# Attention and two MoE layers on one core: first tiles in pieces, squares summed two tiles wide, products planned one matmul at a time

## The chip, the core and the metric

The kernel runs on one core of one Trainium2 chip. The core's engines are TensorE (PE; its weight loads are listed apart as PEld), VectorE (DVE), ScalarE (ACT), GpSimd (POOL, hardly used here) and SyncE (SP, which issues transfers). The metric is the time of one launch on the device in microseconds. Of the kernel before there are three runs: 1128.27 us in the median, 1125.93 to 1128.51.

## What is computed

`q`, `k` and `v` are 6016 x 256 in f32. The attention is over the channels, so its score matrix is only 256 x 256, and its output is the input of two dense layers:

```python
qn = q / (np.linalg.norm(q, axis=1, keepdims=True) + 1e-06)   # norm of each channel, over all tokens
kn = k / (np.linalg.norm(k, axis=1, keepdims=True) + 1e-06)
s = kn.transpose(0, 2, 1) @ qn / tau
a = softmax(s)
x = v @ a                                                     # 6016 x 256
rms = np.sqrt(np.mean(x * x, axis=-1, keepdims=True) + 1e-06)
xn = x / rms * rms_g
g, val = xn @ w_gate, xn @ w_val                              # 1536 wide
y = (silu(g) * val) @ w_out                                   # first MoE
h = y @ w_in                                                  # 2048 wide
out = (h - np.tanh(h)) @ w_out2                               # second MoE
```

## The kernel before

**Attention.** The 6016 tokens are 47 tiles of 128 rows. `attention()` groups them in 12 chunks: the first four tiles in pieces of 1, 1 and 2 tiles (FIRST_PIECES), ten whole chunks of four tiles, and three last tiles as 2 and 1. A tile of q or k is 128 x 256 f32, so a piece of two is 128x512 and a whole chunk 128x1024 in the rows. SP's queue issues all loads of q and those of k but the three pieces of k's first chunk, which go through ScalarE's queue. For each tile and each half m of the channels, `score()` adds one f32 matmul k-tile x q-tile to S[m] in PSUM: 94 matmuls. An f32 matmul leaves two records in the trace, a matmul of the layers below one. Before the first S, TensorE multiplies WARM = 11 dummies of ones into `nrm`. In the last four chunks (BEHIND) all S[0] come first and S[1] last.

**Sums of squares.** The norms need the sum of q^2 and of k^2 over all tokens. ScalarE squares each piece (`sq`); the first chunk goes right into `acc`, [128, 2, 4, 256], four tiles wide for q and for k. VectorE adds every later square to it, 1024 columns in one instruction. Towards the end (FOLDED = 2) it folds `acc` from four tiles to one, and folds the last squares before it adds them. TensorE then multiplies `acc` by ones into `nrm` (two matmuls for q, s = 0, two for k, s = 1). VectorE makes 1/norm of it (n_, y_, t_, r_, 128x8 each), TensorE spreads it (`rq_ps`), and the softmax gives `a`, from which x = v @ a follows.

**Layers.** A layer's hidden columns come in units (6 of the gate and 6 of the value for each of five pairs of token blocks in the first MoE, p = 1 to 5, 30 of each; 48 in the second). `unit()` forms a product of 2 x 2 blocks with seven products, in the PSUM banks X, T, Y and Z: X gets A11*B11, T gets S1*T1, ScalarE copies X to Y and T to m5, Y gets S2*T2, VectorE adds Z = Y + m5, X gets A12*B21, Y gets S3*T3, Z gets S4*B22 and Y gets A22*T4. In the rows a trailing g, v or h names the gate, value or second layer: Yv<-T2h,sh is the first matmul that adds S2*T2 to Y of a value unit, on top of the copy Yv<-Xv. Each product is made of f32 parts, high and low (wh, wl, xh, xl): three matmuls wh*xh, wl*xh, wh*xl of up to 512 columns, in `prod()`. The outputs `acc<-uc` collect the second half of each layer; they fill the time between.

**The order.** A planner in Python (`Graph`) decides it when the kernel is built. Each `g.op` is an instruction with a cost, its operands and, for TensorE, a key; `run()` goes through time with LATENCY between engines, takes on TensorE the ready instruction with the least key, and on the others the one that has to be done first by the round before (`late`); `schedule()` keeps the best of ROUNDS = 6. A `prod` is one instruction of the plan: its three matmuls stand together and it is ready when all four parts are. Each engine then runs its list in order, waiting on semaphores. The field `slack` adds to a transfer's planned end only.

Of the kernel before, what the change touches and what calls it, by code (L numbers as in the profile page):

```python
# [16 lines left out]
P = 128  # L17
# [96 lines left out]
class Graph:  # L114
# [38 lines left out]
    def run(self):  # L153
# [12 lines left out]

        def now_known(o):
            heappush(known[o.eng], (o.ready, o.idx))
            if o.eng != "SP":
                for s, data in o.succs:  # L170
                    if s.left == 1 and s.eng != o.eng and s.eng in PATIENT:
                        soon[s.eng].append((o.ready + o.cost + self.gap(o, s, data), s.idx))
# [113 lines left out]
ROUNDS = 6  # L286
FIRST_PIECES, LAST_PIECES = [1, 1, 2], [2, 1]
FOLDED, BEHIND = 2, 4
WARM = 11
LAG0, LAG1, LAG2 = 4100.0, 9500.0, 4800.0  # L290
# [4 lines left out]
def attn_moe_kernel(  # L295
# [129 lines left out]
    def prod(out, w, x, n, start, key=None):  # L425

        (wh, wl), (xh, xl) = w, x

        def emit():
            o = ap(out)  # L430
            for i, (a, b) in enumerate(((wh, xh), (wl, xh), (wh, xl))):
                nc.tensor.matmul(  # L432
                    o, ap(a), ap(b), start=start and i == 0, stop=i == 2, skip_group_check=True)

        return g.op("PE", 3 * (n / 2.4 + 13.7), emit, [wh, wl, xh, xl], [out], key=key)

    def matmul(out, a, b, n, start, stop, full=True, key=None, **kw):
        return g.op(
            "PE", n * (4 if full else 1) / 2.4 + (5 if full else 13.7),
            lambda: nc.tensor.matmul(ap(out), ap(a), ap(b), start=start, stop=stop, **kw),  # L440
            [a, b], [out], key=key)

    def rsqrt(m, y, t, cols):
# [231 lines left out]
    def attention():  # L675
        CH = 4
        chunks, t = [], 0
        for pieces in [FIRST_PIECES] + [[CH]] * ((NT - CH - sum(LAST_PIECES)) // CH) + [LAST_PIECES]:
            chunks.append((t, [(sum(pieces[:x]), n) for x, n in enumerate(pieces)]))
            t += sum(pieces)  # L680
# [6 lines left out]
        kr = k.rearrange("(p n) c -> p n c", p=P)  # L687
        acc = new(head, "acc", "acc", [P, 2, CH, C])
        S = [bank(ACC[0][m], f"S{m}") for m in range(KC)]
# [3 lines left out]
        def load(i):  # L693
# [3 lines left out]
            for j, n in pieces:  # L697
                for s, src in enumerate((qr, kr)):
                    r, size = raw[i][s], n * C * P * 4
                    from_ = src[:, t0 + j:t0 + j + n, :]  # L700
                    to = r.view(lambda t, j=j, n=n: t[:, j:j + n, :], j)
                    if s and i == 0:
                        g.op("SP", 0, lambda to=to, a=from_: nc.scalar.dma_start(
                            out=to.ap, in_=a), (), [to], size=size)
                    else:
                        last_score[:] = [dma(to, from_, size, (), [to])]
# [18 lines left out]
        for i, (t0, pieces) in enumerate(chunks):  # L725
            load(i)
            sqs = [None] * 2
            if i:
                for s in range(2):
                    pool, tag = ((head, "sq"), (act, "wraw"), (act, "vl"))[(2 * i + s) % 3]  # L730
                    sqs[s] = new(pool, tag, f"sq{i}_{s}", [P, CH, C])
            for j, n in pieces:
                for s in range(2):
                    src = raw[i][s].view(lambda t, j=j, n=n: t[:, j:j + n], j)
                    if i == 0:
                        activation(sums(s, lambda t, s=s, j=j, n=n: t[:, s, j:j + n]), src,
                                   AF.Square, n * C)
                        continue

                    def sq(x, n):  # L740
                        return sqs[s].view(lambda t, j=j: t[:, j + x:j + x + n], j)

                    activation(sq(0, n), src, AF.Square, n * C)
                    if i < NCH - FOLDED:
                        a = sums(s, lambda t, s=s: t[:, s])
                        add(a, a, sq(0, n), n * C)
                        continue
                    for h in (2, 1):
                        if n >= 2 * h:
                            add(sq(0, h), sq(0, h), sq(h, h), h * C)  # L750
                    a = sums(s, lambda t, s=s: t[:, s, 0])
                    add(a, a, sq(0, 1), C)
            if i == NCH - FOLDED - 1:
                for s in range(2):
                    for h in (2, 1):
                        add(sums(s, lambda t, s=s, h=h: t[:, s, :h]),
                            sums(s, lambda t, s=s, h=h: t[:, s, :h]),
                            sums(s, lambda t, s=s, h=h: t[:, s, h:2 * h]), h * C)
            if i < NCH - BEHIND:
# [16 lines left out]
        for s in range(2):  # L776
            for m in range(KC):
                c0 = 2 * (KC * s + m)
                matmul(nrm[:, c0:c0 + 2],
                       sums(s, lambda t, s=s, m=m: t[:, s, 0, m * P:(m + 1) * P]),  # L780
                       ones[:, :2], 2 * 24, True, True, key=0.0)
        n_, y_, t_, r_ = (new(head, x, f"{x}_", [P, NN]) for x in "nytr")
# [10 lines left out]
        for m in range(KC):  # L793
            matmul(rq_ps[:, m * P:(m + 1) * P],
                   r_.view(lambda t, m=m: t[:, 2 * m:2 * m + 1].to_broadcast([P, P])), ident, P,
                   True, True, key=0.0)
        rq = rr("rq")
# [576 lines left out]
```

## Time and profile before

| | us |
|---|---|
| median of 3 runs | 1128.27 |
| lowest, highest | 1125.93, 1128.51 |
| the profiled execution | 1126.14 |
| its span in the trace | 1124.3 |
| TensorE busy | 1118.2 |
| VectorE busy | 815.1 |
| ScalarE busy | 695.2 |

The span is shorter than the execution by 1.84 us. A matmul's record goes on while the next has begun: at 512 columns a record is 0.39 us long, and the next starts about 0.23 us after it. The distance from start to start tells more than the busy time.

### The profile page before, as it was taken

To read this page: it belongs to the slowest core of one execution; us is meant where nothing else is said; L and a number is where in the kernel's file an instruction comes from. 1 tells how busy PE (TensorE), PEld (TensorE's weight loads), DVE (VectorE), ACT (ScalarE), POOL (GpSimd) and SP (SyncE) were. 2 spreads that over 40 slices of the span, in tenths; PEclk is the share of its full clock that TensorE was granted. 3 is DMA by queue.
4 is the path that set the end of the run, shared out by engine and by line. 5 is a ranking of instruction groups with operands and counts; after the bars stand their busy time and mean duration, and the time that the engine had idled before them with its cause. 6 is when DMAs were issued, how large, how long until landed. Compare 5 with 4: busy or idle time off the path is not lost.

```text
span 1124.3 us, 14173 instructions
## 1 busy us (share of the span) xinstructions
PE 1118.2 (99%) x4986; PEld 926.7 (82%) x4986; DVE 815.1 (72%) x1360; ACT 695.2 (62%) x1203; POOL 0.7 (0%) x6
## 2 busy tenths in 40 slices
PE   9999999999999999999999999999999999999998
PEld 8778888878888888888788899888888888888887
DVE  5889866786779578547865877867767768667664
ACT  6675556566656655555655766756656656656654
POOL 0000000000000000000000000000000000000000
PEclk9999999999999999999999999999999999999999
DMA  9765112224332320100221300101100101100101
GB/s 352 288 205 170 57 64 64 67 66 128 116 88 73 113 85 19 56 16 19 72 67 45 92 36 12 59 1 29 47 1 29 48 1 29 38 1 1 38 1 38
DMA packets 41771, 76.74 MB, mean 68 GB/s; under 512 B 6874, under 2 KB 12250, under 8 KB 41700
## 3 DMA queue, kind: packets, MB, share of 16 engines
q1 hardware_dynamic: 41268, 75.31, 20.3%
q8 instruction: 39, 0.64, 0.2%
q10 hardware_dynamic: 432, 0.52, 0.1%
q14 instruction: 32, 0.26, 0.1%
HBM read 54.02 MB, written 21.80 MB: 67 GB/s over the span
## 4 chain that ended last, share of the span: by engine, by line
PE 96%; DMA 3%; DVE 1%; ACT 0%; issue 0%; SPq 0%; ACTq 0%
PE acc L432 40%; PE Yh L432 9%; PE Yv L432 6%; PE Xh L432 6%; PE Yg L432 6%; PE Xg L432 4%; PE Xv L432 4%; PE Zh L432 3%; PE Th L432 3%; PE g L432 3%; PE v L432 3%; DMA q<-q_in 2%; PE x L432 2%; PE Tv L432 2%; PE Tg L432 2%; PE Zv L432 2%
## 5 line engine op out<-in xcount | busy, mean ns | idle before, releaser
L413 DVE TENSOR_TENSOR ulc<-wc,uc 128x512 fp32r<-128x512 f32 (+1 forms) x192 | 130.2, 679 | 89.2 <-ACT uc L394 87.1
L394 ACT ACTIVATE uc<-wc 128x512 fp32r<-128x512 f32 (+1 forms) x192 | 119.6, 624 | 102.0 <-PE acc L432 86.6
L394 ACT ACTIVATE uc<-tc 128x512 fp32r<-128x512 f32 x120 | 73.8, 630 | 99.8 <-DVE tc L409 95.3
L413 DVE TENSOR_TENSOR ulc<-tc,uc 128x512 fp32r<-128x512 f32 x120 | 79.9, 684 | 3.5 <-ACT uc L394 2.6
L409 DVE TENSOR_TENSOR Zv<-Yv,m5v 128x512 f32<-128x512 f32 x30 | 20.9, 696 | 49.3 <-PE Yv L432 49.3
L409 DVE TENSOR_TENSOR wc<-Xh,wc 128x512 f32<-128x512 f32 (+1 forms) x48 | 32.5, 677 | 19.7 <-ACT wc L394 19.4
L394 ACT ACTIVATE wc<-Xh 128x512 f32<-128x512 f32 (+1 forms) x48 | 28.2, 587 | 28.8 <-PE Xh L432 28.6
L440 PE MATMUL S<-q,k 128*128 128x256 f32 x188 | 42.4, 384 | 0.4 <-DMA k<-k_in 0.4
L409 DVE TENSOR_TENSOR Zh<-Yh,m5h 128x512 f32<-128x512 f32 (+1 forms) x48 | 32.9, 686 | 10.8 <-ACT m5h L394 10.4
L440 PEld LDWEIGHTS S<-q,k 128*128 128x128 f32 x188 | 35.8, 193 | 5.8 <-issue 0.8
L409 DVE TENSOR_TENSOR wc<-Yh,wc 128x512 f32<-128x512 f32 (+1 forms) x48 | 32.5, 678 | 9.6 <-ACT wc L394 9.6
L394 ACT ACTIVATE wc<-Yh 128x512 f32<-128x512 f32 (+1 forms) x48 | 28.1, 586 | 14.2 <-PE Yh L432 13.5
L394 ACT ACTIVATE tc<-Xg 128x512 f32<-128x512 f32 x30 | 17.9, 597 | 29.7 <-PE Xg L432 29.7
L394 ACT ACTIVATE m5h<-Th 128x512 f32<-128x512 f32 (+1 forms) x48 | 28.2, 588 | 12.0 <-PE Th L432 12.0
L394 ACT ACTIVATE Yh<-Xh 128x512 f32<-128x512 f32 (+1 forms) x48 | 27.6, 575 | 11.6 <-PE Xh L432 9.7
L394 ACT ACTIVATE r<-acc 128x512 f32<-128x512 f32 (+2 forms) x48 | 27.5, 591 | 9.4 <-PE acc L432 9.0
L409 DVE TENSOR_TENSOR s<-Yh,m5h 128x512 f32<-128x512 f32 (+1 forms) x48 | 32.5, 676 | 0.1
L409 DVE TENSOR_TENSOR acc<-acc,sq 128x1024 f32<-128x1024 f32 (+1 forms) x24 | 24.4, 1023 | 11.1 <-ACT sq L394 10.1
L409 DVE TENSOR_TENSOR wc<-s,wc 128x512 f32<-128x512 f32 (+1 forms) x48 | 32.3, 673 | 0.2
L409 DVE TENSOR_TENSOR wc<-Zh,wc 128x512 f32<-128x512 f32 (+1 forms) x48 | 32.2, 671 | 0.0
L409 DVE TENSOR_TENSOR tc<-Yg,m5g 128x512 f32<-128x512 f32 x30 | 20.6, 687 | 15.9 <-PE Yg L432 15.7
L394 ACT ACTIVATE tc<-Zg 128x512 f32<-128x512 f32 x30 | 17.9, 596 | 23.0 <-PE Zg L432 18.9
(923 smaller groups left out, 3495.1 us busy)
## 6 DMA issues: line engine op xcount, KB each, us to landing
vraw<-vT_in SPq DMA_DIRECT2D x11, 512.0 KB, 5.1
y<-r SPq DMA_DIRECT2D x22, 256.0 KB, 2.0
q<-q_in SPq DMA_DIRECT2D x10, 512.0 KB, 8.7
k<-k_in SPq DMA_DIRECT2D x10, 512.0 KB, 9.4
y<-y SPq DMA_DIRECT2D x20, 256.0 KB, 2.6
outT<-r SPq DMA_DIRECT2D x20, 256.0 KB, 2.0
raw<-w_in_in SPq DMA_DIRECT2D x8, 512.0 KB, 4.4
raw<-w_out_in SPq DMA_DIRECT2D x8, 512.0 KB
```

The costliest lines, as they stand in the source:

```text
L394: nc.scalar.activation(out=ap(out), in_=ap(in_), func=func, **{x: ap(a) for x, a in kw.items()})
L409: return dve(lambda: f(out=ap(out), in0=ap(a), in1=ap(b)), n, 2, [a, b], [out])
L413: lambda: nc.vector.tensor_sub(out=ap(out), in0=ap(in_), in1=f32(ap(hi))), n, 2,
L432: nc.tensor.matmul(o, ap(a), ap(b), start=start and i == 0, stop=i == 2, skip_group_check=True)
L440: lambda: nc.tensor.matmul(ap(out), ap(a), ap(b), start=start, stop=stop, **kw),
```

## The change

`FIRST_PIECES` is a list of three chunks: 1, 1, 2; then 2, 2; then 2, 2. k's piece of two tiles in the first chunk goes to SP's queue. `WARM` is 6. `acc` is two tiles wide; only the first two tiles are squared into it, all others are added two tiles at a time, and no square or sum is folded on VectorE. The `nrm` matmuls are four for q and four for k, in pairs that add the two tiles of `acc`. The first `nrm` matmul of each and the first of `rq_ps` carry a slack of 700, by which the planner takes them for ready later. `prod()` makes three instructions of the plan in place of one, each with only its own two operands.

```diff
@@ now_known
+            if o.eng != "SP":
+                o.ready += o.slack
@@
-FIRST_PIECES, LAST_PIECES = [1, 1, 2], [2, 1]
-FOLDED, BEHIND = 2, 4
-WARM = 11
+FIRST_PIECES, LAST_PIECES = [[1, 1, 2], [2, 2], [2, 2]], [2, 1]
+BEHIND = 4
+WARM = 6
+MARGIN = 700.0
@@ prod
-        def emit():
-            o = ap(out)
-            for i, (a, b) in enumerate(((wh, xh), (wl, xh), (wh, xl))):
-                nc.tensor.matmul(
-                    o, ap(a), ap(b), start=start and i == 0, stop=i == 2, skip_group_check=True)
-        return g.op("PE", 3 * (n / 2.4 + 13.7), emit, [wh, wl, xh, xl], [out], key=key)
+        for i, (a, b) in enumerate(((wh, xh), (wl, xh), (wh, xl))):
+            g.op("PE", n / 2.4 + 13.7, lambda i=i, a=a, b=b: nc.tensor.matmul(
+                ap(out), ap(a), ap(b), start=start and i == 0, stop=i == 2,
+                skip_group_check=True), [a, b], [out], key=key)
@@ matmul
+        o.slack = slack
+        return o
@@ attention
-        acc = new(head, "acc", "acc", [P, 2, CH, C])
+        acc = new(head, "acc", "acc", [P, 2, 2, C])
-                    if s and i == 0:
+                    if s and i == 0 and j < 2:
                         g.op("SP", 0, lambda to=to, a=from_: nc.scalar.dma_start(
@@
+                    def part(x, n):
+                        return sums(s, lambda t, s=s: t[:, s, x:x + n])
@@
                     activation(sq(0, n), src, AF.Square, n * C)
-                    if i < NCH - FOLDED:
-                        a = sums(s, lambda t, s=s: t[:, s])
-                        add(a, a, sq(0, n), n * C)
-                        continue
-                    for h in (2, 1):
-                        if n >= 2 * h:
-                            add(sq(0, h), sq(0, h), sq(h, h), h * C)
-                    a = sums(s, lambda t, s=s: t[:, s, 0])
-                    add(a, a, sq(0, 1), C)
+                    for x in range(0, n, 2):
+                        w = min(2, n - x)
+                        add(part(0, w), part(0, w), sq(x, w), w * C)
@@ nrm
-                matmul(nrm[:, c0:c0 + 2],
-                       sums(s, lambda t, s=s, m=m: t[:, s, 0, m * P:(m + 1) * P]),
-                       ones[:, :2], 2 * 24, True, True, key=0.0)
+                for x in range(2):
+                    matmul(nrm[:, c0:c0 + 2],
+                           sums(s, lambda t, s=s, m=m, x=x: t[:, s, x, m * P:(m + 1) * P]),
+                           ones[:, :2], 2 * 24, x == 0, x == 1, key=0.0,
+                           slack=0 if m or x else MARGIN)
```

TensorE around the norms, as it stands before (S_178 and S_185 are the two halves of S, the tiles named 253 to 292 belong to the last chunks):

```order
L440 MATMUL S_178<-q_253,k_257 128x256 x4
L440 MATMUL S_178<-q_274,k_277 128x256 x2
L440 MATMUL nrm<-ones,acc 128x2 x2
L440 MATMUL S_178<-q_274,k_277 128x256
L440 MATMUL nrm<-ones,acc 128x2 x2
L440 MATMUL S_178<-q_274,k_277 128x256
L440 MATMUL S_178<-q_292,k_296 128x256 x3
L440 MATMUL S_185<-q_233,k_238 128x256 x4
L440 MATMUL S_185<-q_253,k_257 128x256 x4
L440 MATMUL S_185<-q_274,k_277 128x256
L440 MATMUL rq_ps<-ident,r__428 128x128 x2
L440 MATMUL S_185<-q_274,k_277 128x256 x3
```

The same place after (the halves are S_161 and S_168, the last chunks 263 to 307):

```order
L439 MATMUL S_161<-q_263,k_269 128x256 x4
L439 MATMUL S_161<-q_286,k_290 128x256
L439 MATMUL nrm<-ones,acc 128x2 x4
L439 MATMUL S_161<-q_286,k_290 128x256 x2
L439 MATMUL nrm<-ones,acc 128x2 x4
L439 MATMUL S_161<-q_286,k_290 128x256
L439 MATMUL S_161<-q_307,k_313 128x256 x3
L439 MATMUL S_168<-q_243,k_246 128x256 x4
L439 MATMUL S_168<-q_263,k_269 128x256 x2
L439 MATMUL rq_ps<-ident,r__438 128x128 x2
L439 MATMUL S_168<-q_263,k_269 128x256 x2
L439 MATMUL S_168<-q_286,k_290 128x256 x4
```

q's sums stand one S matmul earlier and are four matmuls instead of two; two S matmuls instead of one stand between q's and k's; the spread `rq_ps` has ten S matmuls between it and k's sums instead of thirteen.

VectorE in the chain from the norms to their reciprocal, before (gv0y and w10y are weights of the layers being prepared, 1024 wide):

```order
L461 SCALAR_TENSOR_TENSOR t__399<-y__394,n__392 128x8
L464 TENSOR_TENSOR t__399<-t__399,y__394 128x8
L526 TENSOR_SCALAR gv0y<-gv0y 128x1024
L465 SCALAR_TENSOR_TENSOR y__394<-t__399,y__394 128x8
L531 SCALAR_TENSOR_TENSOR gv0y<-gv0raw,gv0y 128x1024
L786 TENSOR_TENSOR y__394<-y__394,n__392 128x8
L536 SCALAR_TENSOR_TENSOR gv0y<-gv0raw,gv0y 128x1024
L787 TENSOR_SCALAR y__394<-y__394 128x8
L788 TENSOR_SCALAR y__394<-y__394,tau_t 128x4
L790 RECIPROCAL r__428<-y__394 128x8
```

And after:

```order
L462 SCALAR_TENSOR_TENSOR t__418<-y__415,n__413 128x8
L465 TENSOR_TENSOR t__418<-t__418,y__415 128x8
L466 SCALAR_TENSOR_TENSOR y__415<-t__418,y__415 128x8
L781 TENSOR_TENSOR y__415<-y__415,n__413 128x8
L782 TENSOR_SCALAR y__415<-y__415 128x8
L783 TENSOR_SCALAR y__415<-y__415,tau_t 128x4
L527 TENSOR_SCALAR gv0y<-gv0y 128x1024
L785 RECIPROCAL r__438<-y__415 128x8
L532 SCALAR_TENSOR_TENSOR gv0y<-gv0raw,gv0y 128x1024
L537 SCALAR_TENSOR_TENSOR gv0y<-gv0raw,gv0y 128x1024
```

The three wide instructions on gv0y stood between the short ones; two of them now stand behind the reciprocal, and the first just ahead of it.

TensorE in a unit of the second MoE (X is A11\*B11, T is S1\*T1, Y gets S2\*T2 on the copy of X), before:

```order
L432 MATMUL Xh_7976<-B11l,l20h 128x512
L432 MATMUL acc_7399<-uc_7891,l26h 128x512
L432 MATMUL acc_7399<-uc_7891,l26l 128x512
L432 MATMUL acc_7399<-ulc_7898,l26h 128x512
L432 MATMUL acc_7405<-uc_7891,l26h 128x512
L432 MATMUL acc_7405<-uc_7891,l26l 128x512
L432 MATMUL acc_7405<-ulc_7898,l26h 128x512
L432 MATMUL Th_7998<-T1h,l2s_5104 128x512 x2
L432 MATMUL Th_7998<-T1l,l2s_5104 128x512
L432 MATMUL Yh_7987<-T2h,l2s_5104 128x512 x2
L432 MATMUL Yh_7987<-T2l,l2s_5104 128x512
```

And in a unit after:

```order
L432 MATMUL Xh_8443<-B11l,l25h 128x512
L432 MATMUL Th_8460<-T1h,l2s_5786 128x512 x2
L432 MATMUL Th_8460<-T1l,l2s_5786 128x512
L432 MATMUL acc_8128<-uc_8406,l24h 128x512
L432 MATMUL Yh_8464<-T2h,l2s_5786 128x512 x2
L432 MATMUL Yh_8464<-T2l,l2s_5786 128x512
L432 MATMUL Xh_8443<-B21h,l25h 128x512
L432 MATMUL Xh_8443<-B21h,l25l 128x512
L432 MATMUL Xh_8443<-B21l,l25h 128x512
L432 MATMUL acc_8128<-uc_8406,l24l 128x512
L432 MATMUL acc_8128<-ulc_8415,l24h 128x512
L432 MATMUL Yh_8464<-T3h,l25h 128x512
```

Between the last matmul of X with B11 and the first of Y with T2 there were six outputs and three of T; in this unit of after there are three of T and one output, and five matmuls between Y's last with T2 and its first with T3.

## Rows read from the trace of the kernel before

**Rows 1.** The page: busy time of engines, chain that ended last.
```profile
PE 1118.2 (99%) x4986; PEld 926.7 (82%) x4986; DVE 815.1 (72%) x1360; ACT 695.2 (62%) x1203; POOL 0.7 (0%) x6
...
PE 96%; DMA 3%; DVE 1%; ACT 0%; issue 0%; SPq 0%; ACTq 0%
```

**Rows 2.** By stage: window, length, busy, granted clock, DMA share, GB/s.
```profile
0.00:5.94 5.94, 4.86 (x22) 4.86 (x23) 0.54 (x3) 2.63 (x5) 0.70 (x6) 1.00 0.60 188
...
10.72:39.07 28.35, 28.35 (x131) 24.98 (x132) 26.32 (x29) 21.85 (x23) 0.00 (x0) 1.00 1.03 400
...
155.50:633.90 478.40, 478.33 (x2082) 387.90 (x2081) 338.72 (x596) 288.78 (x511) 0.00 (x0) 1.00 0.23 70
```

**Rows 3.** Waits of TensorE and its weight load: total, times, longest, us.
```profile
PE nrm L440 <- DVE ones L483: 1.1, 1, 1.1
PE nrm L440 <- DVE acc L409: 0.9, 1, 0.9
PE S L440 <- DMA k<-k_in: 0.4, 1, 0.4
...
PEld Yv L432 <- ACT Yv L394: 7.1, 17, 0.5
...
PEld Yg L432 <- ACT Yg L394: 1.2, 5, 0.3
...
PEld Yh L432 <- DVE Zh L409: 0.9, 4, 0.3
```

**Rows 4.** TensorE's timeline of the head: start, duration, idle before.
```profile
1.08 5.07 PE L440 MATMUL nrm<-ones 128*128 128x128 f32 x22 [1.08 <-DVE ones L483]
5.94 4.34 PE L440 MATMUL S<-q,k 128*128 128x256 f32 x16
10.72 28.73 PE L440 MATMUL S<-q,k 128*128 128x256 f32 x132 [0.44 <-DMA k<-k_in]
40.31 0.61 PE L440 MATMUL nrm<-ones,acc 128*128 128x2 f32 x4 [0.86 <-DVE acc L409]
40.78 0.68 PE L440 MATMUL S<-q,k 128*128 128x256 f32 x2
```

**Rows 5.** ScalarE's timeline of the squares, first and last.
```profile
4.38 0.40 ACT L394 ACTIVATE acc<-k 128x256 f32<-128x256 f32 x1
7.96 0.63 ACT L394 ACTIVATE acc<-q 128x512 f32<-128x512 f32 x1 [3.18 <-DMA q<-q_in]
8.50 0.61 ACT L394 ACTIVATE acc<-k 128x512 f32<-128x512 f32 x1
...
35.78 1.14 ACT L394 ACTIVATE sq<-q 128x512 f32<-128x512 f32 x2
```

**Rows 6.** VectorE's timeline of the fold.
```profile
33.27 0.69 DVE L409 TENSOR_TENSOR acc<-acc 128x512 f32<-128x512 f32 x1
...
39.84 1.28 DVE L409 TENSOR_TENSOR acc<-acc,sq 128x256 f32<-128x256 f32 x3
```

**Rows 7.** One of 17 stalls: ScalarE, weight load and TensorE, 241 to 244.
```profile
242.12 0.58 ACT L394 ACTIVATE Yv<-Xv 128x512 f32<-128x512 f32 x1
...
242.75 0.19 PEld L432 LDWEIGHTS Yv<-T2h,sh 128*128 128x128 f32 x1 [0.41 <-ACT Yv L394]
...
242.75 0.50 PE L432 MATMUL Yv<-T2h,sh 128*128 128x512 f32 x1
```

**Rows 8.** A unit of the second MoE, 767 to 772.
```profile
767.26 0.39 PE L432 MATMUL Xh<-B11l,l26h 128*128 128x512 f32 x1
...
767.68 0.58 ACT L394 ACTIVATE Yh<-Xh 128x512 f32<-128x512 f32 x1 [0.27 <-PE Xh L432]
...
769.98 0.39 PE L432 MATMUL Yh<-T2l,l2s 128*128 128x512 f32 x1
...
770.48 0.70 DVE L409 TENSOR_TENSOR Zh<-Yh,m5h 128x512 f32<-128x512 f32 x1 [0.30 <-ACT m5h L394]
...
771.57 0.39 PE L432 MATMUL Yh<-T3h,l26h 128*128 128x512 f32 x1
```

More of the change, by code (lines that the diff above doesn't have):

```diff
@@ L427, in prod, with matmul @@
         (wh, wl), (xh, xl) = w, x
-        def emit():
-            o = ap(out)
-            for i, (a, b) in enumerate(((wh, xh), (wl, xh), (wh, xl))):
-                nc.tensor.matmul(
-                    o, ap(a), ap(b), start=start and i == 0, stop=i == 2, skip_group_check=True)
-        return g.op("PE", 3 * (n / 2.4 + 13.7), emit, [wh, wl, xh, xl], [out], key=key)
-    def matmul(out, a, b, n, start, stop, full=True, key=None, **kw):
-        return g.op(
+        for i, (a, b) in enumerate(((wh, xh), (wl, xh), (wh, xl))):
+            g.op("PE", n / 2.4 + 13.7, lambda i=i, a=a, b=b: nc.tensor.matmul(
+                ap(out), ap(a), ap(b), start=start and i == 0, stop=i == 2,
+                skip_group_check=True), [a, b], [out], key=key)
+    def matmul(out, a, b, n, start, stop, full=True, key=None, slack=0, **kw):
+        o = g.op(
             "PE", n * (4 if full else 1) / 2.4 + (5 if full else 13.7),
@@ L677, in attention @@
         chunks, t = [], 0
-        for pieces in [FIRST_PIECES] + [[CH]] * ((NT - CH - sum(LAST_PIECES)) // CH) + [LAST_PIECES]:
+        whole = (NT - len(FIRST_PIECES) * CH - sum(LAST_PIECES)) // CH
+        for pieces in FIRST_PIECES + [[CH]] * whole + [LAST_PIECES]:
             chunks.append((t, [(sum(pieces[:x]), n) for x, n in enumerate(pieces)]))
@@ L727, in attention @@
             sqs = [None] * 2
[L728 to L731, printed above, removed]
+            for s in range(2):
+                pool, tag = ((head, "sq"), (act, "wraw"), (act, "vl"))[(2 * i + s) % 3]
+                sqs[s] = new(pool, tag, f"sq{i}_{s}", [P, CH, C])
             for j, n in pieces:
@@ L734, in attention @@
                     src = raw[i][s].view(lambda t, j=j, n=n: t[:, j:j + n], j)
-                    if i == 0:
-                        activation(sums(s, lambda t, s=s, j=j, n=n: t[:, s, j:j + n]), src,
-                                   AF.Square, n * C)
+                    def part(x, n):
+                        return sums(s, lambda t, s=s: t[:, s, x:x + n])
+                    if i == 0 and j < 2:
+                        assert n == 1
+                        activation(part(j, 1), src, AF.Square, C)
                         continue
                     def sq(x, n):
-                        return sqs[s].view(lambda t, j=j: t[:, j + x:j + x + n], j)
+                        return sqs[s].view(lambda t, x=j + x: t[:, x:x + n], j)
                     activation(sq(0, n), src, AF.Square, n * C)
-                    if i < NCH - FOLDED:
-                        a = sums(s, lambda t, s=s: t[:, s])
-                        add(a, a, sq(0, n), n * C)
-                        continue
-                    for h in (2, 1):
-                        if n >= 2 * h:
-                            add(sq(0, h), sq(0, h), sq(h, h), h * C)
-                    a = sums(s, lambda t, s=s: t[:, s, 0])
-                    add(a, a, sq(0, 1), C)
[L753 to L758, printed above, removed]
+                    for x in range(0, n, 2):
+                        w = min(2, n - x)
+                        add(part(0, w), part(0, w), sq(x, w), w * C)
             if i < NCH - BEHIND:
@@ L795, in attention @@
                    r_.view(lambda t, m=m: t[:, 2 * m:2 * m + 1].to_broadcast([P, P])), ident, P,
-                   True, True, key=0.0)
+                   True, True, key=0.0, slack=0 if m else MARGIN)
         rq = rr("rq")
```

## The prediction, made before the changed kernel had run

> **What bounds the kernel now.** I read the page first. TensorE is busy 99% of the span and holds 96% of the chain that ended last; VectorE and ScalarE are at 72% and 62% [rows 1]. So only two things can move the end: the number and length of TensorE's own records, and the few places where it stands. The second view is the one by stage [rows 2]: in the first MoE (155.5 to 633.9 us) TensorE is busy 478.33 of 478.40 us, so busy time cannot show what is lost there, since a matmul whose weights come late counts as busy. A longer record shows it. That is why I read the waits third, of TensorE and of its weight load apart [rows 3]: TensorE has three waits in all, 1.1 us for the first constant, 0.9 for the sum of squares, 0.4 for k; the weight load waits 7.1 us for ScalarE's copy of Yv, 17 times, and some 2 us in two other short ones. Fourth come the timelines of the head [rows 4 to 6]: dummies from 1.08, S from 5.94, `nrm` at 40.31. All sums are made against the profiled execution, 1126.14 us (span 1124.3, 1.84 around it); the median of the runs is 1128.27, and a difference found here is put on 1128.27.
>
> **Fewer dummies, pieces.** First the clock. 22 dummy records of 128 columns take 5.94 - 1.08 = 4.86 us, 0.221 each; an f32 record of S has 256 columns and takes 28.73/132 = 0.218 [rows 4]. So the dummies run at the lower level, 1.2 GHz, and S later at 2.4, though the column of the granted clock says 1.00 for both stretches [rows 2]. A record of S at the low level is taken as twice 0.218, 0.43. With 12 dummy records S can start at 1.08 + 12 x 0.221 = 3.73; its operands are there by then or just behind (ScalarE squares k1, the last of the first two tiles, at 4.38 with three squares queued ahead of it [rows 5]). Tiles 0 and 1 are 8 records: 3.4 us, done at 7.2. Then S needs q2 and k2. They were squared at 7.96, after 3.18 us of waiting for the DMA, and at 8.50 [rows 5]. The same bytes are ahead of them after, so I take k2 at 8.3, and TensorE stands about 1.1 us there. In before it stood again for the first whole chunk's k, till 10.72 [rows 4]; that chunk now comes in halves, the first needing half the bytes, so I expect S to run on from 8.3. 138 S records stand between this and `nrm`: 8.3 + 138 x 0.218 = 38.4, against 10.72 + 28.73 = 39.45 in before. That is 1.1 us earlier, of which 0.43 is one S matmul that now stands behind `nrm`.
>
> **The sums of squares.** In before TensorE then waited 0.86 us for `acc` and started `nrm` at 40.31 [rows 4], since VectorE was folding: its last three short adds alone run from 39.84 to 41.12 [rows 6]. After, a whole square needs two 512-wide adds of at most 0.69 [rows 6], 1.38 together with their start-up, and arrives every 512 KB / 400 GB/s = 1.31 us [rows 2]; VectorE is about level with it, without folds. The last q squares end at 35.78 + 1.14 = 36.9 [rows 5]; behind them I count one add of k's chunk (0.69) and q's own last one (0.43, a third of 1.28): 38.1. Small transfers are slower: the first stage moved 188 GB/s at a busy share of 0.60, so 313 at full share, the later one 400 at 1.03 [rows 2]. For the 2 MB of the next two chunks in half pieces I take 350 for 388, 0.6 us more at most. So q's `nrm` can start at 38.2 to 38.8 (an estimate). The fold is paid on TensorE: 16 records for 8, at (40.78 - 40.31)/4 = 0.117 each [rows 4], +0.9 us, and the S matmul left behind is 0.43. Equal to before is thus a start at 40.31 - 1.35 = 38.96. Gain 0.2 to 0.7; I take **-0.3**, with +0.6 (TensorE stands again for a piece) and -1.3 (pieces land by 7.2) as ends. The chain n, y, t to `rq` loses the wide instructions on gv0y and MARGIN puts `rq_ps` three S matmuls earlier; TensorE has no wait there [rows 3], since S is there to fill, so both are 0. So is the product of g that now stands ahead of the last `ms` at the gate's start: no wait of TensorE is listed there either.
>
> The Trainium skill, DMA: Bandwidth & Descriptors, section Rules for kernel authors, speaks against the pieces: for most bandwidth it wants large transfers, 1 MiB and over. The halves are 256 KB; the 313 against 388 GB/s above agrees in its direction. By that rule the head would lose the 0.6 us.
>
> **Products matmul by matmul.** No arithmetic goes. What changes is which matmuls stand between a result and the product that needs it. The copy of Xv to Yv takes ScalarE 0.58 us from 242.12; the load of T2h starts at 242.75, 0.05 after its end, and its matmul is recorded 0.50 long where others have 0.39 [rows 7, 8]: a load that itself waits is not hidden and costs 0.11. The copy starts 0.03 after X's matmul ends (767.26 + 0.39 to 767.68 [rows 8]). So from the start of X's last matmul, Y needs 0.39 + 0.03 + 0.58 + 0.05 + 0.11 = 1.16 us; n matmuls between give (n + 1) x 0.227 (769.98 to 771.57 is seven [rows 8]). n = 4 is short by 0.03 to 0.04, n = 5 is enough. By the order, 45 of 48 units of the second MoE have n = 9 in before; after, 29 have n = 4 and 7 have 5. That is 29 x 0.04 = 1.2 us. In the gate units n goes from 6 to 4 at 10 of 30 places, 0.4; seven others, 0.3. The second chain is VectorE's: Y's last matmul with T2 at 769.98, Zh from 770.48 to 771.18, and T3 may not write before it is read: 0.39 + 0.11 + 0.70 + 0.05 + 0.11 = 1.36 us. This unit of before has n = 6 there and T3 follows at 771.57 without loss [rows 8]; after, about 130 places over h, g and v have n = 5, 1.36 us: 0 to 0.015 each, 1.0 in sum. The 17 stalls of Yv stay: at 17 places six matmuls still stand between the last of Yg with T4 and Yv with T2, and in that time ScalarE has to do a silu of Yg and then the copy. So +2.9 (an estimate from these durations and the order), less what the other short waits of the weight load, 1.2 and 0.9 [rows 3], give back; I take 0.9: **+2.0**, with 0 and +6 as ends.
>
> The skill's page TensorE: Matmul & The Clock Gate, Part 2, says TensorE's queue pulls weight loads ahead of matmuls in flight, so that the next tile's weights load while this tile's matmul runs. By that alone the 0.11 would be nothing at any place; the record of 0.50 us [rows 7] says that this fails where the load's own wait ends late.
>
> **Sum.** -0.3 + 2.0 = +1.7 us: 1127.8 for the profiled execution, **1130.0** on the median. What a measurement of this kernel can tell from no change is about 0.3%, 3.4 us; so the forecast is no difference.
>
> **The rivals.**
> A, faster: the head gives its whole 1.3, and the finer products end Yv's 17 stalls. These are worth between 17 x 0.11 = 1.9 and the whole 7.1 us of [rows 3], part of which lies under running matmuls; the middle is 4.5. For it: they are the largest wait, and a finer plan can put X's last part earlier. Against: the order of after has six matmuls between at the same count of places. It gives 1128.27 - 1.3 - 4.5 = 1122.5.
> B, slower: each of the some 175 new tight places exposes its weight load. Half of 0.11 each is 9.6 us in place of 2.0: 1128.27 - 0.3 + 9.6 = 1137.6. For it: the margins are 0.00 and -0.04 us, and any other instruction of ScalarE or VectorE (0.58 to 0.70 us) that is in the way falls on TensorE at once, where before had 0.2 to 1.1 us to spare. Against: ScalarE stood idle for 0.27 us before the copy in [rows 8], and the planner laid these engines' queues. It decides from about 0.026 us a place (4.6, less 0.3 and 0.9).
> C, the change doesn't do what it says in the head: `nrm` still waits for the last landing, and the fold costs its 0.9 us on top: +0.9 to +1.2 there, with the products some 1131.3 in all.
> D, the clock: with ten dummy records less, TensorE stands about 1.1 us before q2. If it stays at the lower level for the next eight records, each takes 0.43 for 0.22: +1.7 us, of which the wait for `acc` takes about half, so 1130.9. No row shows such a stand at the low level, other than before's own, ended at 10.72, behind which the records took 0.218 [rows 4]. The page on the clock gate, Part 1, says the default state is throttled and activity releases it; that speaks for D.
>
> **How the numbers follow.** No measurable change 0.66 (the sum, and C and D with small products). A 0.10. B, and the sum together with C or D beyond +3.4, 0.24. The range: down to 1125.5 (head 1.3, products 0, a third of Yv's stalls gone), up to 1134 (products +6, nothing won in the head), which leaves out the far halves of A and B.
>
> **What would show it.** S from 3.7, then about 1 us of idle time between 7.2 and 8.3 that names q or k; `nrm` between 38.2 and 39.0; x 0.2 to 0.6 us earlier than before. The weight load's waits for ACT Yh new, some 30 of them, Yh with T2h longer than 0.39 at about 29 of 48, and Yv's waits still near 17, so that the loss is spread over both MoEs. It is wrong if S runs on without a stand, if Yv's 17 waits are gone, or if the stage from 634 us on is over 4 us longer.

## The result, and the profile after

The changed kernel takes 1135.93 us in the median (1133.51 to 1138.63, five runs), against 1126.95 (1125.93 to 1128.51) for the kernel before. The ratio is 1.0076, with a 95% interval from 1.0055 to 1.0098. The forecast was 1130.0, within 1125.5 to 1134.0, and no measurable difference. It became slower by 9.0 us, near rival B, which stood 9.3 above the median of its time (1137.6 on 1128.27), and not the likeliest case, +1.7. The median under the forecast was that of three runs; with the five here it is 1.3 lower.

The profiled execution took 1134.19 us with a span of 1132.4. From the starts of the first g, Xg and Xh in each trace, and the end of TensorE's last matmul, the program falls into four stretches (us); 3.6 us follow behind the last one in before and 3.8 after:

| kernel | to the first g | gate, to Xg | first MoE, to Xh | second MoE |
|---|---|---|---|---|
| before | 67.99 | 87.27 | 478.24 | 487.24 |
| after | 66.00 | 88.48 | 482.26 | 491.87 |

The head won 2.0 us, the gate lost 1.2, and the two MoEs lost 4.0 and 4.6. One matmul of the mean square, 0.34 us, moved from the first stretch into the second; up to Xg, 0.8 us are won. The page shows nothing of this: TensorE is busy 99% as in [rows 1], with two records fewer.

```profile
span 1132.4 us, 14207 instructions
...
PE 1126.3 (99%) x4984; PEld 915.4 (81%) x4984; DVE 817.3 (72%) x1372; ACT 694.9 (61%) x1207; POOL 0.7 (0%) x6
```

By stretch (window, length, then busy time of TensorE, its weight load, VectorE, ScalarE, GpSimd, granted clock, share of the DMA engines, GB/s), the MoEs after are simply longer while TensorE counts as busy all the time, as it did in [rows 2]:

```profile
154.48:636.74 482.26, 482.20 (x2081) 382.39 (x2080) 340.63 (x594) 288.22 (x512) 0.00 (x0) 1.00 0.23 69
636.74:1128.60 491.86, 491.86 (x2185) 403.73 (x2183) 347.83 (x543) 309.31 (x545) 0.00 (x0) 1.00 0.07 24
```

What names the loss is the view of the weight load's waits (us in total, times, longest), to be read beside [rows 3]. Yv's waits for ScalarE stayed (18 for 17). New are 37 waits of Yh for the same engine, 21 of Yg where there were 5, and 30 for VectorE's Zh and Zg where Zh had 4 and Zg one:

```profile
PEld Yh L432 <- ACT Yh L397: 7.5, 37, 0.3
PEld Yv L432 <- ACT Yv L397: 7.4, 18, 0.5
...
PEld Yg L432 <- ACT Yg L397: 4.1, 21, 0.3
PEld Yh L432 <- DVE Zh L412: 3.0, 15, 0.2
PEld Yg L432 <- DVE Zg L412: 2.7, 15, 0.2
```

One of these places in the second MoE, in TensorE's timeline (start, duration; with one output between T and Y, so n = 4). Its weight load waited for ScalarE's copy:

```profile
742.22 0.39 PE L432 MATMUL Th<-T1l,l2s 128*128 128x512 f32 x1
742.45 0.39 PE L432 MATMUL acc<-uc,l22h 128*128 128x512 f32 x1
742.67 0.66 PE L432 MATMUL Yh<-T2h,l2s 128*128 128x512 f32 x2
743.17 0.40 PE L432 MATMUL Yh<-T2l,l2s 128*128 128x512 f32 x1
743.40 0.40 PE L432 MATMUL Xh<-B21h,l23h 128*128 128x512 f32 x1
743.64 0.39 PE L432 MATMUL Xh<-B21h,l23l 128*128 128x512 f32 x1
743.86 0.39 PE L432 MATMUL Xh<-B21l,l23h 128*128 128x512 f32 x1
744.10 0.40 PE L432 MATMUL acc<-uc,l22l 128*128 128x512 f32 x1
744.33 0.39 PE L432 MATMUL acc<-ulc,l22h 128*128 128x512 f32 x1
744.56 0.40 PE L432 MATMUL Yh<-T3h,l23h 128*128 128x512 f32 x1
744.80 0.40 PE L432 MATMUL acc<-uc,l22h 128*128 128x512 f32 x1
745.03 0.39 PE L432 MATMUL acc<-uc,l22l 128*128 128x512 f32 x1
```

```profile
742.23 0.19 PEld L432 LDWEIGHTS acc<-uc,l22h 128*128 128x128 f32 x1
742.60 0.30 PEld L432 LDWEIGHTS Yh<-T2h,l2s 128*128 128x128 f32 x2 [0.19 <-ACT Yh L397]
742.94 0.19 PEld L432 LDWEIGHTS Yh<-T2l,l2s 128*128 128x128 f32 x1
```

The two matmuls from 742.67 take 0.50 us to the next one, 0.04 more than two undisturbed. That is the price that the prediction gave the place. But it doesn't end there: most of the following ones start 0.23 to 0.24 us apart instead of 0.2265, down to 745.03. By the records' own starts the eleven matmuls from the late load on lost 0.096 us in all. Elsewhere in this trace a load starts 0.22 us ahead of its matmul; here it started 0.075 ahead. The Trainium skill, TensorE: Matmul & The Clock Gate, Part 2, says that TensorE's queue pulls loads ahead of matmuls in flight. The rows agree where the load has nothing to wait for, and the late one shows what is lost when it has.

### The profile page after: what moved, and what is told of

Read it like the earlier page. It is cut to its first block, busy times and chain, and to the rows that moved or that the text cites. A ratio compares the mean times of both kernels' runs of the same rounds, so it can differ in the third digit from the quotient of the medians.

```text
span 1132.4 us, 14207 instructions
## 1 busy us (share of the span) xinstructions
PE 1126.3 (99%) x4984; PEld 915.4 (81%) x4984; DVE 817.3 (72%) x1372; ACT 694.9 (61%) x1207; POOL 0.7 (0%) x6
## 4 chain that ended last, share of the span: by engine, by line
PE 94%; DMA 3%; DVE 2%; ACT 1%; issue 0%; SPq 0%; ACTq 0%
PE acc L432 40%; PE Yh L432 9%; PE Yv L432 6%; PE Xh L432 6%; PE Yg L432 6%; PE Xv L432 4%; PE Xg L432 4%; PE Zh L432 3%; PE Th L432 3%; DMA k<-k_in 2%; PE x L432 2%; PE v L432 2%; PE Tv L432 2%; PE Zg L432 2%; PE Zv L432 2%; PE Tg L432 2%
## 5 line engine op out<-in xcount | busy, mean ns | idle before, releaser
L397 ACT ACTIVATE wc<-Zh 128x512 f32<-128x512 f32 (+1 forms) x48 | 28.2, 588 | 27.3 <-PE Zh L432 27.3
L397 ACT ACTIVATE wc<-s 128x512 f32<-128x512 f32 (+1 forms) x48 | 29.9, 623 | 15.8 <-DVE s L412 15.6
L432 PE MATMUL Zh<-B22h,l2s 128*128 128x512 f32 (+1 forms) x96 | 35.7, 386 | 0.0
L412 DVE TENSOR_TENSOR acc<-acc,sq 128x512 f32<-128x512 f32 (+1 forms) x46 | 29.4, 677 | 8.3 <-ACT sq L397 7.6
L432 PE MATMUL acc<-uc,w10h 128*128 128x512 f32 x80 | 31.3, 393 | 0.0
L432 PE MATMUL acc<-uc,w12l 128*128 128x512 f32 x80 | 31.2, 390 | 0.0
```

The source lines that it names most:

```text
L397: nc.scalar.activation(out=ap(out), in_=ap(in_), func=func, **{x: ap(a) for x, a in kw.items()})
L412: return dve(lambda: f(out=ap(out), in0=ap(a), in1=ap(b)), n, 2, [a, b], [out])
L432: g.op("PE", n / 2.4 + 13.7, lambda i=i, a=a, b=b: nc.tensor.matmul(ap(out), ap(a), ap(b), start=start and i == 0, stop=i == 2, skip_group ...
```

## The experiments

Theory M: the loss comes from weight loads that end late at new tight places, and a late load costs more than its own lateness, since the matmuls behind it are longer too. Rivals: another part of the change makes the MoEs slower (O); matmuls that change output and weights from one to the next cost something of themselves (I). The head is a question of its own: which of its parts brought the gain.

The time of a kernel goes with its mean granted clock: the kernel before took 1125.3 to 1127.6 us at 0.999 or 1.000, and 1127.7 to 1130.9 at 0.996 to 0.998. Where a difference of 1 to 2 us decides, the median of the executions at 0.999 and above is given too ("full clock"): 1126.4 to 1126.8 for before and 1133.85, of two executions, for after. The last section comes back to this.

**Products whole again.** From the changed kernel, `prod` goes back to one instruction of the plan:

```diff
-        for i, (a, b) in enumerate(((wh, xh), (wl, xh), (wh, xl))):
-            g.op("PE", n / 2.4 + 13.7, lambda i=i, a=a, b=b: nc.tensor.matmul(
...
+        return g.op("PE", 3 * (n / 2.4 + 13.7), emit, [wh, wl, xh, xl], [out], key=key)
```

> The changed kernel with one part undone: a product is again one instruction of the plan (its three matmuls together), the head stays as changed. By the order, 44 of 48 units of the second MoE have nine matmuls again between X's last and Y's first with T2, and 42 have six between T2 and T3. Theory M (margins: the loss comes from weight loads that end late at the new tight places): the two MoEs go back to their lengths in the kernel before, 478 and 487 us, and the head keeps its gain of 1.2 to 2.0 us, so about 1125.0 us, against 1126.95 before, ratio 0.998. Theory O (the loss comes from another part of the change, such as the buffers that the first tiles take): the MoEs stay 3 to 4 us longer each, 1134 or more. A third reading, that the head's gain is given back at the gate (its stage was 1.2 us longer): 1126.5 to 1127.

Measured: 1128.45 us, ratio 0.9999 (0.9984 to 1.0014). The first MoE took 478.84 us and the second 487.21, the lengths of the kernel before, as M says and O doesn't. No weight load of Yh waits for ScalarE there. The median missed the expected 1125.0: seven of twelve runs had a granted clock of 0.995 to 0.997 and took 1128.4 to 1130.4. The five at full clock took 1124.65. So the head's parts are worth 1.75 us at full clock with whole products, and the split costs all the rest.

**Split alone.** From the kernel before, only `prod` as in the change:

> The kernel before with one part done alone: a product is three instructions of the plan; the head is as before. The counts between X, Y and T3 are those of the changed kernel (29 units with four, 42 with five). Theory M: first MoE some 4 us and second some 4.6 us longer than before, 1126.95 + 8.6 to 10 = 1135.5 to 1137. Theory O: within 2 us of the kernel before.

Measured: 1137.04 us, ratio 1.0083 (1.0066 to 1.0099), 1135.5 at full clock; MoEs 482.65 and 492.37. The split alone costs 9.1 us at full clock, and 9.1 less 1.75 is the change's 7.4. O is out. The waits of Yh are there again:

```profile
PEld Yh L429 <- ACT Yh L394: 7.8, 37, 0.4
```

**Later readiness for both engines.** From the changed kernel, two numbers of the planner; the products stay split:

```diff
-    ("ACT", "PE"): 152, ("DVE", "PE"): 140, ("DVE", "ACT"): 120, ("ACT", "DVE"): 132,
+    ("ACT", "PE"): 252, ("DVE", "PE"): 340, ("DVE", "ACT"): 120, ("ACT", "DVE"): 132,
```

> The changed kernel with two numbers of the planner: a result of ScalarE is planned for TensorE 100 ns later (252 for 152), one of VectorE 200 ns later (340 for 140). By the order no unit of the second MoE has four matmuls between X and Y (28 have five, 12 six) and 41 have six between T2 and T3, where five stood; the 17 places of Yv in the first MoE have seven where six stood. The products are still interleaved matmul by matmul. Theory M: nearly all late loads go, Yv's 17 too: second MoE 487 to 488 us, first 474 to 477, in all 1119 to 1123. Theory I (interleaving itself costs: outputs and weights that change from matmul to matmul, or contention): the second MoE stays at 490 to 492 and the time above 1131.

Measured: 1123.67 us, ratio 0.9967 (0.9954 to 0.998), 1122.2 at full clock. MoEs 474.83 and 489.29. The order is as fine as in the changed kernel, and 11.6 us are gone, so I is out as the main cause. The median is just above the expectation and the value at full clock in it. What is left is in the second MoE, 2 us longer than with whole products. Ten loads of Yh still waited for ScalarE, and 28 units have five matmuls between X and Y; but 1.0 of the 2 us is in two unbroken rows of 448-column matmuls that start slightly further apart (last section).

```profile
PEld Yv L432 <- ACT Yv L397: 4.6, 21, 0.5
...
PEld Yh L432 <- ACT Yh L397: 2.5, 10, 0.3
```

**One engine at a time.** The same with ScalarE's number alone (252), and with VectorE's alone (340):

> As the run with both numbers, but only ScalarE's results are planned 100 ns later. Four becomes five between X and Y, Yv's 17 places have seven or more, and VectorE's chain keeps five between T2 and T3 (39 of 48). Theory M with the late load of Y as the whole cause in the second MoE (39 of 49 stretches of longer spacing begin there, 0.145 us each, 5.6 in sum): second MoE 488 us, in all 1121 to 1125. If VectorE's chain at five has a share of its own of some 0.01 us at each of 130 places plus what follows, 1 to 3 us more. Theory I: above 1131.

> The changed kernel; only VectorE's results are planned 200 ns later for TensorE (340 for 140). By the order T3 has six or more behind T2 nearly everywhere, but 29 units of the second MoE keep four between X and Y, and Yv's 17 places keep six. With both planned later the time at the full clock was 1122.2, with ScalarE's alone 1126.6, with neither 1133.9. Theory M with the two chains adding up: 11.7 of gain less 7.3 leaves 4.4 for this one, so 1129.5 at the full clock, the second MoE between 489 and 491 us, and Yh's load still waiting for ScalarE at about 29 places. If a late load of Y were the whole cause: 1133 to 1134, as the changed kernel.

Measured: ScalarE's alone 1127.17 us (1.0004, 0.999 to 1.0018), 1126.55 at full clock; VectorE's alone 1132.21 (1.0052, 1.0039 to 1.0065), 1131.9. The first lies above the 1121 to 1125 of a late Y as the whole cause, by no more than the 1 to 3 us that the text gave VectorE's chain; the second lies between its two expectations, 1129.5 and 1133 to 1134. From 1133.85 these are 7.3 and 2.0, and both together 11.6, so the two don't add up: VectorE's margin is worth 2.0 while ScalarE's loads are late and 4.3 once they aren't. The waits of the kernel with ScalarE's number show it. Yh's loads for ScalarE went from 37 to 5; VectorE's Zh took their place with 39 waits, as many as units with five matmuls between T2 and T3:

```profile
PEld Yh L432 <- DVE Zh L412: 6.9, 39, 0.3
...
PEld Yg L432 <- DVE Zg L412: 3.4, 18, 0.3
PEld Yv L432 <- ACT Yv L397: 3.1, 13, 0.5
...
PEld Yh L432 <- ACT Yh L397: 1.2, 5, 0.2
```

**The head's parts.** From the kernel before, the pieces and the six dummies alone, and the sums alone (two tiles wide, fold on TensorE, slack):

> The kernel before with one part done alone: the first twelve tiles in pieces, k's third piece on SyncE's queue and six dummies for eleven; the squares are added and folded as before, products are whole. At the full clock the kernel before takes 1126.4 and the one with all of the head's parts 1124.65. Theory H1 (the pieces bring S forward and the sums are what TensorE then waits for): S runs on without a stand, nrm waits 1.5 to 2.5 us for the fold on VectorE, and little is won: 1126.0 to 1126.6. Theory H2 (the pieces are the gain): 1124.6 to 1125.

> The kernel before with the other part of the head alone: squares added two tiles at a time, the fold on TensorE, and the slack on the norms; first four tiles in pieces only, eleven dummies, products whole. Theory H1: the wait for acc shrinks from 0.9 to 0 to 0.5 us, 0.9 us of nrm records come on top, so about 1126; with the pieces alone and this the two do not add up to the 1.75 of both. Theory H2: 1126.4 or a little above. Either way S starts at 5.4 to 6 and stands for the first whole chunk's k.

Measured: pieces and dummies 1125.0 us (0.9991, 0.9983 to 1.0), 1124.9 at full clock; sums 1127.71 (1.0004, 0.9993 to 1.0016), 1125.75. At full clock the pieces bring 1.5 to 1.6 and the sums 0.6 to 0.7, where both together bring 1.75; the sums' executions there (1125.25 to 1127.49) spread as widely as those of before (1125.4 to 1127.3), so their part isn't clear of noise. H2 holds on the size: the pieces are most of it. H1 holds on the wait: in the profiled execution of the pieces, TensorE stood 2.50 us for `acc`. This run also moves k's third piece to SyncE's queue, so the pieces' size and the queue aren't told apart.

**Eleven dummies with the pieces.** From the kernel with both numbers later:

```diff
-WARM = 6
+WARM = 11
```

> As the run with both engines' results planned later (1123.7 in the median, 1122.2 at the full clock), with eleven dummies for six; the pieces stay. S starts at 5.9 for 3.8 and should run on without a stand; nrm is held by acc in either case, so at the full clock 1122 to 1122.6: the dummies that were taken out are worth nothing there, the pieces are. If the earlier start of S is the gain: 1123.5 or more. The wait for acc shrinks from 1.1 to some 0.3 us.

Measured: 1127.96 us, ratio 1.0001 (0.9991 to 1.001). A miss: none of its eleven executions had a granted clock of 0.999. S started at 5.33 in the profiled one and ran on without a stand, but TensorE then stood 1.61 us for `acc`, not 0.3, and behind `nrm` S ran at the lower level. What the dummies cost by themselves can't be told from it.

**Norms later.** From the kernel with both numbers later, q's and k's first `nrm` matmul with more slack:

```diff
-                           slack=0 if m or x else MARGIN)
+                           slack=0 if m or x else 1500.0)
```

> The run in which both engines' results are planned later, with the norms' slack at 1500 for 700 (the spread keeps 700): q's nrm matmuls stand behind two more S matmuls. There TensorE stood 1.12 us for acc; now 0.3 us or less. Theory C (in about half of the executions the clock falls to the lower level behind this stand, as in two profiled ones, where S records took 0.427 us for several us behind nrm): with the stand gone, the granted clock is 0.999 or 1.000 in nearly all runs, where it was lower in 6 of 12, and the median comes to 1122 from 1123.7. Rival (the clock falls for another reason, or because of the short records of nrm themselves): as many runs below 0.999 as before, median 1123 to 1124.

Measured: 1122.0 us, ratio 0.9959 (0.9947 to 0.9971); four of five runs at 0.999 or above. S runs on to `nrm` without a wait (37.78), though x then waits 0.58 us for `a`. As theory C expected, but five runs are few, and the split kernel of the next paragraph speaks against it: with the same slack and no stand at `nrm` in its profile, three of five runs were at 0.998.

**Six matmuls between, and whole products with the same numbers.** The norms later and ScalarE's number at 460; then the same with whole products:

> As the run with the norms later (median 1122.0, second MoE 488.4 us in its profile), with ScalarE's results planned another 208 ns later (460 for 252). By the order no unit of the second MoE has fewer than six matmuls between X and Y (28 had five), and Yv's places have eight (seven). Theory M: a chain of 1.16 us should already fit into five matmuls' 1.36; where it did not (ten loads of Yh still waited, 2.7 us), ScalarE had another instruction in the way, and 0.23 us more lets most of these go too: second MoE 486 to 487 us, first 473 to 474, median 1118 to 1120.5. Rival: what is left (3.3 and 3.7 us of longer spacing) doesn't come from these loads: 1121.5 to 1122.5.

> As the run with six between, but a product is again one instruction of the plan. By the order X to Y has nine or more in the second MoE, T2 to T3 six, and Yv's places nine where six stood. If the split as such gives nothing (the gain over the kernel before comes from the planner's later readiness and the head alone): within 1 us of the run with six between, 1118 to 1121. If the finer order is worth something once the loads are in time: 1 to 3 us slower than it, for the seventeen places of Yv above all.

Measured: split 1121.01 us (0.9937, 0.9923 to 0.995), MoEs 472.22 and 487.73; whole 1119.81 (0.9927, 0.9912 to 0.9942), MoEs 473.41 and 486.84. The split version misses its expectation by 0.5 us (1120.3 at full clock), and its loss in the second MoE is down to 0.5 us against the kernel before, not gone. The whole one is the fastest kernel here, 7.5 us below the runs of before beside it (7.0 at full clock). The split as such is worth nothing once loads are in time: at full clock it is 0.5 us slower. In the waits of the whole one, Yv's 17 have become one:

```profile
PEld Yv L435 <- DVE Zv L412: 0.5, 2, 0.3
...
PEld Yv L435 <- ACT Yv L397: 0.5, 1, 0.5
```

**The two numbers alone.** From the kernel before, 460 and 340 and nothing else:

> The kernel before with the two numbers of the planner alone (ScalarE's results 460 for 152, VectorE's 340 for 140); head and products as before. By the order 17 places of Yv have nine or more matmuls where six stood. If the gain of the best kernel so far (1119.8) is the sum of the two parts, the later readiness is worth 1119.8 + 1.8 (the head's part at the full clock, 1126.4 to 1124.65) = 1121.6, with the first MoE some 473 us for 478; if the head with its norms later is worth more, 1122 to 1124.

Measured: 1122.09 us, ratio 0.9963 (0.995 to 0.9977), first MoE 472.94 for 478.24, second 486.97. It comes within 0.5 us of the expectation, in part by luck: that was reckoned at the full clock, and all five runs had 0.997 or 0.998. In the profiled one (1120.94), x and r from 59.63 to 64.01 ran at the lower level and took 4.38 us, where the changed kernel took 2.69 for the same records. Without that it would have taken some 1119.3 (an estimate), no more than the 1120.03 of the fastest kernel's profiled execution. By this estimate nearly all of the fastest kernel's gain at the full clock comes from two numbers of the planner that the change left as they were; that the head's parts add to it there is not shown.

## Why the prediction was wrong

**The clock and the dummies: right.** S started at 3.81 (3.73 forecast), in eight records mostly 0.427 us apart. It didn't stay there: rival D did not happen at this place. In before, too, the first two distances of S were 0.427, and in the other eight traces with six dummies the lower level ended after one to eight records.

**The pieces: a step failed.** "Then S needs q2 and k2 ... TensorE stands about 1.1 us there" put q2 and k2 at 8.3, from the rows of before, since the same bytes were ahead of them. ScalarE squared them at 6.18 and 6.95 after, for 7.96 and 8.50 in [rows 5], and the next half chunk followed at 7.61 (ScalarE's timeline after):

```profile
6.18 0.63 ACT L397 ACTIVATE sq<-q 128x512 f32<-128x512 f32 x1 [1.16 <-DMA q<-q_in]
6.95 0.63 ACT L397 ACTIVATE sq<-k 128x512 f32<-128x512 f32 x1
7.61 0.63 ACT L397 ACTIVATE sq<-q 128x512 f32<-128x512 f32 x1
```

In before, the transfers behind q2 and k2 were whole chunks, and after they are halves; that q2 and k2 shared the DMA engines with what came behind them is argued from this, not measured, and k2's other queue is a rival that no run tells from it. TensorE ran through from 3.81 until it stood for `acc`:

```profile
1.08 2.93 PE L439 MATMUL nrm<-ones 128*128 128x128 f32 x12 [1.08 <-DVE ones L484]
3.81 33.44 PE L439 MATMUL S<-q,k 128*128 128x256 f32 x146
38.07 1.05 PE L439 MATMUL nrm<-ones,acc 128*128 128x2 f32 x8 [0.83 <-DVE acc L412]
38.99 1.11 PE L439 MATMUL S<-q,k 128*128 128x256 f32 x4
...
49.47 2.88 PE L439 MATMUL x<-vraw,a 128*128 128x512 f32 x7
```

That it ran through is in part luck of this execution: in six of the other eight traces with the same pieces and six dummies, S was faster at the start and TensorE stood 0.20 to 1.25 us for k. But S's ninth record started at 6.55 to 7.40 in all nine, and at 8.13 to 8.38 in the four without the pieces. With the pieces and eleven dummies it was 7.06, so the dummies don't explain it. The forecast, 8.3, is the time without the pieces.

**The sums: right in kind, small in size.** `nrm` started at 38.07, still held by `acc` for 0.83 us, 0.13 before the range of 38.2 to 38.8. Against the tie at 38.96 that is 0.9 us, and x, at 49.47, is 1.2 us earlier than in before. The head's forecast of -0.3 (-1.3 at best) was -1.75 at full clock, with whole products; in the profiled pair it is -0.8 up to Xg.

**The gate: small miss.** x and its sums to the first g gained another 0.8, and 1.2 were lost to the first Xg; 0.34 of both is the matmul of the mean square that moved. The forecast had 0 for both; the net is +0.4. About as long TensorE now stands for ScalarE's t before one product of g (waits after):

```profile
PE g L432 <- ACT t L397: 0.4, 1, 0.4
```

**The products: the step that decided.** The count of places between X and Y was right: 29 with n = 4 and 7 with n = 5, beside 37 waits of Yh, and Yv's 17 stayed at 18. The direct price was right as well, though its own terms give 0.025 (1.16 less 5 x 0.227): 27 of the places in the second MoE lose just 0.040 us in the first distance. Nine more lose 0.08 to 0.11 there, where the load came later still. Three things failed.

First, "n = 4 is short by 0.03 to 0.04" took this for the whole price. With the longer distances behind it a place mostly loses 0.09 to 0.12 us over 11 to 17 matmuls. Undisturbed matmuls start 0.2265 us apart at 512 columns and 0.203 in the mean at 448. Beyond these, the second MoE lost 0.7 us in before and 5.3 after, and 4.7 of the 5.3 are in 40 stretches that begin at Y's first matmul with T2 or the one ahead of it. In the first MoE the same sum went from 7.5 to 11.6, above all at the gate's Yg.

Second, "a load that itself waits ... costs 0.11" read only the record's own length. The matmul of [rows 7] also starts late. TensorE in before:

```profile
242.15 0.39 PE L432 MATMUL acc<-uc,w12l 128*128 128x512 f32 x1
242.37 0.39 PE L432 MATMUL acc<-ulc,w12h 128*128 128x512 f32 x1
242.75 0.50 PE L432 MATMUL Yv<-T2h,sh 128*128 128x512 f32 x1
243.09 0.40 PE L432 MATMUL Yv<-T2h,sl 128*128 128x512 f32 x1
243.33 0.40 PE L432 MATMUL Yv<-T2l,sh 128*128 128x512 f32 x1
```

It starts 0.38 us behind the one before it, 0.15 too late; the next follows 0.11 too late; and with the tail behind it the stall costs 0.30, which the busy time hides. Seventeen of these are 5.1 us (an estimate), about what the first MoE won with the two numbers of the planner alone (478.24 to 472.94).

Third, "less what the other short waits ... give back; I take 0.9": nothing came back, the waits for Yg and Zh grew threefold.

So +2.0 was 9.1 measured (split alone, full clock). Rival B came near it with 9.6, in part by luck: it took half of 0.11 for each of 175 places, and of these "about 130 places" with five matmuls between T2 and T3 the trace shows only 92 (42 of h, 24 of g, 26 of v). Two of the prediction's own signs of being wrong came true: S ran on without a stand, and the second MoE is over 4 us longer.

**Rival A** is out: the 17 stalls stayed, as the order had said. **Rival C** is out too: the head won.

## What to carry to other kernels

A planner's latency from one engine's result to the next engine's use should be checked against a trace. Here the weight load starts 0.05 us after ScalarE's copy ends [rows 7], and an undisturbed load starts 0.22 us ahead of its matmul; together 0.27 us (an estimate from these rows), where the planner had 0.152. With whole products nine matmuls stood between X and Y in 45 of 48 units of the second MoE, so this showed mostly at Yv's 17 places; the finer plan put four there in 29 units and used the margin up. When instructions are split so that they can start earlier, count the places that then have less than the measured chain. In this kernel a late weight load cost two to three times what the first distance behind it shows. Moving the two numbers brought more than the head's parts did: 1122.1 us alone and 1119.8 with the head and the norms later, against 1126.6 and 1127.4 for before beside them; the clock falls of the first make up most of the difference between the two (an estimate, above).

## What the hardware showed that was not expected

**A late weight load has a tail.** Undisturbed matmuls of 512 columns are recorded 0.389 us long and start 0.2265 apart, the load 0.22 ahead. Behind a late load most are 0.393 to 0.398 long and 0.228 to 0.237 apart, for 11 to 17 matmuls in the second MoE after, without any wait. Matmuls of 448 columns mostly start 0.199, 0.207 and three times 0.203 apart in turn, 0.203 in the mean, in before as after. In the kernel with both numbers later, and in the one with eleven dummies, 31 and then some 263 of them in unbroken rows were 0.206 or 0.207 apart, 1.0 us in sum; the first row begins with Yh's matmuls with T2. With the norms later and the same counts in the second MoE this did not happen. What ends the tail was not tried.

**The clock falls in the middle of the head.** In five of the fourteen profiled executions S, x or r ran at the lower level, 1.2 GHz, for some microseconds after S had once reached 2.4 GHz. Four of them show it at `nrm`, where S then ran slowly, after stands for `acc` of 1.30 us (products whole), 1.88 (split alone), 2.50 (pieces alone) and 1.61 (eleven dummies). In the other ten traces the stand there was 1.12 us or less, and S kept 2.4 GHz behind it. With the pieces alone the granted clock fell at 39.24, still within the stand; in the other three it fell behind the first matmuls of `nrm`. The kernel with eleven dummies, and the changed one beside it, by window from 38 to 46 us (granted clock third from the right, 0.57 and 1.00):

```profile
38.00:46.00 8.00, 8.00 (x30) 6.88 (x30) 4.24 (x16) 2.25 (x2) 0.00 (x0) 0.57 0.84 307
```

```profile
38.00:46.00 8.00, 7.93 (x46) 7.28 (x47) 5.71 (x19) 2.48 (x3) 0.00 (x0) 1.00 0.88 317
```

A second place is behind the two-column matmuls of the mean square (the kernel with products whole has it too, from 62.63): with the two numbers alone, x from 59.63 on took 3.35 us for four records of 512 columns, at a granted clock of 0.66 from 59 to 64, and nothing had waited. In the other twelve traces the clock did not fall at this place:

```profile
57.43 1.10 PE L440 MATMUL x<-vraw,a 128*128 128x512 f32 x2
58.37 1.40 PE L440 MATMUL ms<-mean,sq 128*128 128x2 f32 x12
59.63 3.55 PE L440 MATMUL x<-vraw,a 128*128 128x512 f32 x4
62.98 1.20 PE L440 MATMUL r<-ident,naryb 128*128 128x128 f32 x8
```

```profile
59.00:64.00 5.00, 5.00 (x19) 2.94 (x20) 3.33 (x6) 2.92 (x4) 0.00 (x0) 0.66 0.07 28
```

The fastest kernel, with no stand at `nrm`, had five of five runs at a granted clock of 1.000, within 0.4 us of each other; its split twin, without a stand there too, had three of five at 0.998. The Trainium skill, TensorE: Matmul & The Clock Gate, Part 1, says that the default state is throttled and that activity releases it. The rows agree in that a stand, matmuls of few columns, or both come before the falls; why the same program falls in one execution and not in another (two of the kernel after's five runs did not) stays open.
